# Turning a weight matrix with VectorE and SBUF moves instead of TensorE, in a fused state-space and feed-forward kernel

## The chip, the cores and the metric

The kernel runs on one core of a Trainium2 chip. The metric is the device time of one execution, in microseconds (us). A core has five engines that run side by side: TensorE (PE in the profile; its weight loads are shown apart as PEld), VectorE (DVE), ScalarE (ACT), GpSimd (POOL) and SyncE (SP), which only issues transfers. Sixteen DMA engines carry the transfers that SP, ACT and POOL issue. Matmuls write into PSUM, which has eight banks of 512 f32 numbers on each of 128 partitions; SBUF is the working memory.

## The reference

Two branches of the same input size are mixed by a gate. All sizes: 2048 tokens, model width 448, feed-forward width 1792, state width 448 (complex).

```python
Lam_bar = exp(dt * Lam)                                  # per state lane
Bu   = einsum("bld,pd->blp", x, B_bar)                   # complex
h[t] = Lam_bar * h[t-1] + Bu[t]                          # along 2048 tokens
y    = 2 * einsum("blp,dp->bld", hseq, C).real + x * Dskip
b    = silu(x @ w1) @ w2
g    = sigmoid((x * gate_w).sum(-1))
out  = g * y + (1 - g) * b
```

Inputs and output are bf16. Both branches and the gate take the same x (`A_x`); `B_x` is not used.

## The kernel before

**Tiling.** The tokens are cut into 4 chunks (tc) of 512, and each chunk into 4 blocks (tb) of 128. Weights and x lie in SBUF with the contracted dimension on the partitions. Model width 448 is held as four pieces that overlap (columns 0, 128, 256 and 320), so that products with x use 64-row halves of TensorE, two at a time, into a pair of PSUM banks (line 663). There are two kinds of such product tiles: "F" (x times w1, 14 tiles of 128 features per chunk), which ScalarE evicts with silu into `aT` (line 634), and "B" (x times the turned B, 7 tiles or "slots" per chunk: real and imaginary parts of 448 state lanes), which are copied into a buffer `U`, by VectorE for chunk 0 (line 640) and by ScalarE for the others (line 642). Slot 3 holds 64 lanes of the real and 64 of the imaginary part; two small moves by POOL make its swapped copy, slot 7.

**The recurrence** (`lanes`, line 704 and on). Each lane rotates: the complex recurrence becomes a real one by multiplying U with cosines and sines of the lane's phase (three steps of VectorE: a product with COS into `H`, products with SIN into `PI`, a sum), a scan along the 512 tokens per slot (line 736, into the f32 tile `Gf`), and the rotation back (products with SIN into `PO`, with COS into `H`, a difference). Between scan and rotation back, `Gf` is written as bf16 over U: by POOL transfers (line 390) for chunks 0 to 2, by ScalarE (line 746) for chunk 3. `gin` carries the state into the next chunk. For chunk 0, the first rotation is cut by slot into 18 small steps.

**The readout.** `CP` holds C turned and scaled by the parameters, 7 slots of 128 lanes x 448 columns. For each block, seven matmuls of H with CP (line 795) give y in one PSUM bank, and VectorE adds g times y to `Tb` (line 798), which by then holds g * x * Dskip (line 849) plus the second branch; SP stores the result (line 801). CP is made in `readout_weights`: for each of four slots, 16 TensorE transposes of 56 rows of C (line 814; 64 in all) into a pair of PSUM banks, one or two scaled copies by ScalarE into `ct` (lines 822, 825), and one or two sums by VectorE into CP (lines 827, 830). C itself lies in `H2C`, the space of H of chunk 2, and B in that of chunk 3.

**The second branch.** `ffn2` contracts aT with w2, 14 matmuls per block (line 774); ScalarE scales by 1 - g into `fe` (line 780), and a POOL transfer that accumulates adds fe to Tb (line 782).

**Gates** (`gates`): two products by VectorE, four sums along the row by ScalarE (line 842), tanh and scalings, four scaled copies (line 849).

**The order of the work.** Every operation is recorded with what it reads and writes, a cost and a priority. `Plan.order` then lists it: TensorE keeps the order in which its operations were recorded; each other engine takes, among its operations that could begin soonest, the one with the best priority; PSUM banks are given out in this listing too. The listing fixes each engine's program, and semaphores are placed where one engine needs another. All loads are issued by SP in order (the first few also by ACT): x of chunk 0, w1, parameters, B, gate and Dskip, x of chunk 1, w2, C, x of chunks 2 and 3. The recorded order for TensorE, in short (G is `ffn2`, C the readout, cp the turning of C, xt the turning of x by TensorE, line 508):

```python
x_products(F(0, 0, NH) + B(0) + F(0, NH) + B(1), ...)
for f in cp(0) + G(0, 1) + cp(1, 2) + G(2, 3) + cp(3):
    f()
x_products(F(1) + F(2, 0, 1) + B(2), {2: xt(2, "aa")})
for f in G(4, 5, 6, 7) + C(0, 1, 2, 3):
    f()
x_products(F(2, 1) + B(3) + F(3), {1: xt(3, "aa"), 9: [lambda: gates(3), lambda: lanes(3)]})
for f in C(4, 5, 6, 7) + G(8, 9, 10, 11):
    f()
for f in C(8, 9, 10, 11) + G(12, 13, 14, 15) + C(12, 13, 14, 15):
    f()
```

Of the kernel before, what the change touches and what calls it, by code (L numbers as in the profile page):

```python
# [7 lines left out]
ALU = mybir.AluOpType  # L8
# [6 lines left out]
S_TOK = 2048  # L15
# [9 lines left out]
NFILL = 2  # L25
XCOL = [0, 128, 256, 320]
# [22 lines left out]
class Op:  # L49
    __slots__ = ("i", "eng", "fn", "reads", "writes", "cost", "prio", "sem",  # L50
                 "deps", "succ", "ps_w", "ps_r", "start", "end", "bytes", "tag", "own")


class Plan:
# [5 lines left out]
    RATE = {"pool": 300e3, "hw": 300e3}  # L60
    LAP = {"dve": 0.08, "act": 0.09}
# [6 lines left out]
    def add(self, eng, fn, reads=(), writes=(), cost=0.2, prio=50, sem=None, nbytes=0, tag=""):  # L68
# [28 lines left out]
        o.own = False  # L97
        o.start = o.end = None
# [5 lines left out]
    def order(self):  # L104
# [14 lines left out]
        def earliest(o):  # L119
            t = 0.0  # L120
# [23 lines left out]
        while len(done) < len(ops):  # L144
# [5 lines left out]
            for eng, lst in cands.items():  # L150
# [9 lines left out]
                o = min((c for c in cand if c[0] <= t0 + 1e-9), key=lambda c: (c[1].prio, c[1].i))[1]  # L160
# [116 lines left out]
def bass_gated_mix__ssm_conv_s5__dense_activation_silu__prompt_kernel(nc, A_x, A_Lambda_re, A_Lambda_im, A_B_re, A_B_im, A_C_re, A_C_im,  # L277
               A_log_dt, A_Dskip, B_x, B_w1, B_w2, gate_w, out):
    with ExitStack() as ctx:
# [9 lines left out]
        xT = sb("xT", [128, 4, S_TOK], BF16)  # L289
# [9 lines left out]
        H2C = sb("H2C", [128, 3840], BF16)  # L299
        H = [H2C[:, 0:3584].rearrange("p (s n) -> p s n", s=NSLOT) if k == 2 else sb(f"H{k}", [128, NSLOT, CH], BF16) for k in range(4)]  # L300
        Cnat = H2C[:, :].rearrange("p (b l) -> p b l", b=4)
        cnn = [f"H2_{s}" for s in range(7)] + ["H2_3i"]
# [91 lines left out]
        def load_w1(q, k, a, b):  # L394

            cols = slice(w1cuts[k], w1cuts[k + 1])
            src = B_w1[320:448, cols] if a == 3 else B_w1[128 * a:128 * b, cols].rearrange("(b p) f -> p b f", p=128)
            load(q, w1s[:, 3, cols] if a == 3 else w1s[:, a:b, cols], src, " ".join(f"w1_{k}_{i}" for i in range(a, b)),
                 256 * (b - a) * (cols.stop - cols.start))
# [11 lines left out]
        Bnat = H[3][:, :, 0:D_MOD]  # L411
        load("sp", Bnat[:, 0:3, :], A_B_re[0:384, :].rearrange("(b p) d -> p b d", p=128), "H3_0 H3_1 H3_2", 384 * 896)
        load("sp", Bnat[0:64, 3, :], A_B_re[384:448, :], "H3_3", 64 * 896)
        load("sp", Bnat[64:128, 3, :], A_B_im[384:448, :], "H3_3i", 64 * 896)
        load("sp", Bnat[:, 4:7, :], A_B_im[0:384, :].rearrange("(b p) d -> p b d", p=128), "H3_4 H3_5 H3_6", 384 * 896)
        btn = {s: [f"BT{s}_{h}" for h in range(2)] for s in range(7)}
        load_w1("sp", len(w1cuts) - 2, 0, 3)
        load_w1("sp", len(w1cuts) - 2, 3, 4)
# [8 lines left out]
        def load_C():  # L427

            for h in range(2):
                rows = lambda a: a[224 * h:224 * h + 224, :].rearrange("(b p) l -> p b l", p=56)  # L430
                to = Cnat[64 * h:64 * h + 56]
                load("sp", to[:, :, 0:448], rows(A_C_re), f"Cn0{h} " + (" ".join(cnn) if h == 0 else ""), 224 * 896)
                load("sp", to[:, :, 576:960], rows(A_C_im[:, 0:384]), f"Cn1{h}", 224 * 768)
                load("sp", to[:, :, 448:512], rows(A_C_im[:, 384:448]), f"Cn2{h}", 224 * 300)
                load("sp", to[:, :, 512:576], rows(A_C_re[:, 384:448]), f"Cn3{h}", 224 * 300)
# [32 lines left out]
        def x0_transposes(q0, part, who):  # L468
# [12 lines left out]
            for h in range(2):  # L481
                src = lambda h=h: bk(tk, h).bitcast(BF16)[:, 0:256].rearrange("p (q b n) -> p q b n", q=2, n=64)
                dst = xT[:, q0:q0 + 2, 256 * part:256 * part + 256].rearrange("p q (b h n) -> p q b h n", h=2, n=64)[:, :, :, h, :]
# [11 lines left out]
        xn_of = {tc: {q: [f"xT{tc}_{h}" for h in range(2)] for q in range(4)} for tc in range(1, NCH)}  # L495
        xn_of[0] = {q: [f"xT0_{q}{part}{h}" for part in range(2) for h in range(2)] for q in range(4)}

        def x_transposes(tc, who):
# [13 lines left out]
            for h in range(2):  # L512
                src = lambda h=h: bk(tk, h).bitcast(BF16).rearrange("p (q b n) -> p q b n", q=4, b=4)
                dst = xT[:, :, tc * CH:(tc + 1) * CH].rearrange("p q (b h n) -> p q b h n", h=2, n=64)[:, :, :, h, :]
                if who[h] == "d":
                    DVE(lambda e, src=src, dst=dst: e.tensor_copy(dst, src()), [tk], [f"xT{tc}_{h}"], 0.69, 2.2, "xTe")
                else:
                    ACT(lambda e, src=src, dst=dst: e.activation(dst, src(), AF.Copy), [tk], [f"xT{tc}_{h}"], act_cost(1024), 2.2, "xTe")

# [73 lines left out]
        def b_transposes(s0, s1, who):  # L593
# [12 lines left out]
            PE(mm, [f"H3_{s}" for s in range(s0, s1)] + ["H3_3i"] * (s0 <= 3 < s1) + ["ident"], [tk], n * 4 * 0.0285, "BT")  # L606
# [16 lines left out]
        def evict(pair, tk):  # L623

            kinds = [t[0] for t in pair]
            for k, n in ((0, 2),) if pair[0][:2] == pair[-1][:2] and len(pair) == 2 else ((0, 1), (1, 1))[:len(pair)]:
# [10 lines left out]
                U, un = UG[tc % 2], f"U{tc % 2}_"  # L637
                dst = U[:, sl, :]
                if tc == 0:
                    DVE(lambda e, src=src, dst=dst: e.tensor_copy(dst, src()), [tk], [f"{un}{m}" for m in names], 0.15 + 0.53 * n, 2.6, "U")  # L640
                else:
                    ACT(lambda e, src=src, dst=dst: e.activation(dst, src(), AF.Copy), [tk], [f"{un}{m}" for m in names], act_cost(512 * n), 5, "U")  # L642
# [4 lines left out]
        def x_products(tiles, fill={}, wait=()):  # L647
# [10 lines left out]
            def steps(k, h, a, z):  # L658
                def body(pe):
                    for n, cut in list(enumerate(part[h]))[a:z]:  # L660
                        for b, ((i, p0), tile) in enumerate(zip(cut, pairs[k])):
                            tc = tile[1]
                            r = pe.matmul(bk(toks[k], b), weights(tile, p0, p0 + 64, i), xT[p0:p0 + 64, i, tc * CH:(tc + 1) * CH],  # L663
# [42 lines left out]
        def lanes(tc):  # L706
            pr = 20 + tc
            A, an = H[tc], f"H{tc}"
            U, u = UG[tc % 2], f"U{tc % 2}_"
            Gb = U  # L710
            t = f"L{tc}"
            if tc == 0:
# [20 lines left out]
            for s in (3, 0, 4, 1, 5, 2, 6) if tc else (0, 4, 1, 5, 2, 6, 3):  # L733
# [8 lines left out]
                for dst, src, name in cuts:  # L742
                    if tc + 1 < NCH:
                        load("pool", dst, src, name, 180000, 1, [f"Gf{s}"])
# [23 lines left out]
        def ffn2(tb):  # L768
# [13 lines left out]
            P.add("pool", lambda e: e.dma_start(Tb[:, tb, :], f[:, :], accum_op=ALU.add), [fn, f"Tb{tb}"], [f"Tb{tb}"], 0.94, 2, sem(), 115000, tag="Tb+")  # L782

        outs = [sem() for _ in range(NOT)]

        def readout(tb):
# [3 lines left out]
            for n, (a, b) in enumerate(cuts):  # L790
                tk = Ps()

                def mm(pe, tk=tk, a=a, b=b):
                    for s in range(NSLOT):
                        r = pe.matmul(bk(tk)[:, 0:b - a], H[tc][:, s, o:o + 128], CP[:, s, a:b], start=(s == 0), stop=(s == NSLOT - 1))  # L795
                    return r
                PE(mm, [f"H{tc}_{s}" for s in range(7)] + [f"CP{s}" for s in range(NSLOT)], [tk], NSLOT * (0.0025 + (b - a) / 2400), f"C{tc}")
# [5 lines left out]

        def readout_weights(k):

            tk = Ps(2)

            def mm(pe):
                for j, c0 in ((0, 128 * k), (1, 448 if k == 3 else 576 + 128 * k)):
                    for b in range(4):  # L810
                        o = j * 224 + 56 * b
                        for h in range(2):
                            p = slice(64 * h, 64 * h + 56)
                            r = pe.transpose(bk(tk, h).bitcast(BF16)[:, o:o + 56], Cnat[p, b, c0:c0 + 128], ident[p, p])  # L814
                return r
            PE(mm, [f"Cn{n}{h}" for n in range(4) for h in range(2)] + cnn + ["ident"], [tk], 8 * 0.0285, "CT")
# [102 lines left out]
```

## Time and profile before

| | before |
|---|---|
| median of 3 runs | 141.22 us (141.2 to 141.76) |
| profiled execution | 141.25 us |
| its span in the trace | 139.5 us |
| TensorE clock granted, mean | 0.998 |

The times are of whole executions. The profile is of one execution; its span runs from the first to the last instruction in the trace, so it is a little shorter than the execution's own time. Busy time of an engine is the time in which it had an instruction under way. A line such as L663 is a line of the kernel, and a group of instructions is named by line, engine, operation and the tiles that it writes and reads.

### The profile page before, as it was taken

Reading aid. Unit: us, or ns where it says so; the run is one execution under the profiler, and the core shown is the slowest. Engines: PE = TensorE matmul, PEld = TensorE weight load, DVE = VectorE, ACT = ScalarE, POOL = GpSimd, SP = SyncE. Lnnn points to the kernel's source line nnn. Section 1 sums busy time; section 2 is a strip of 40 time slices with the busy share of each in tenths; the row PEclk is TensorE's granted clock in tenths of the full one; section 3 lists DMA queues with packets and bytes.
Section 4 is the critical chain, followed back from the end, with each engine's and each line's share of the span. In section 5 each row is a group of like instructions: output and inputs, shape, how many; then the busy total and the mean of one; then the engine's idle time right before and its main releaser. Section 6 shows DMA issues by size and latency. Waiting matters only on the chain.

```text
span 139.5 us, 3000 instructions
## 1 busy us (share of the span) xinstructions
PE 135.9 (97%) x1201; PEld 67.0 (48%) x1201; DVE 122.0 (87%) x179; ACT 90.3 (65%) x157; POOL 39.2 (28%) x72
## 2 busy tenths in 40 slices
PE   7999999999999999999999999999999999999992
PEld 2445454455544544455544544444455555555561
DVE  0319999999999999999999999999999999997053
ACT  3349768999989999823694887799931268312300
POOL 7134040100248440227733001824000314022220
PEclk9999999999999999999999999999999999999999
DMA  4998999510156770104976200674202322323242
GB/s 136 337 294 243 363 320 238 177 42 0 31 79 94 129 110 1 38 15 73 157 131 155 38 5 0 95 133 79 38 4 97 66 33 36 83 83 61 40 94 71
DMA packets 17956, 14.71 MB, mean 105 GB/s; under 512 B 2835, under 2 KB 17814, under 8 KB 17942
## 3 DMA queue, kind: packets, MB, share of 16 engines
q0 software_dynamic: 6064, 5.51, 24.8%
q1 hardware_dynamic: 11318, 8.65, 20.7%
q10 hardware_dynamic: 560, 0.36, 0.8%
q8 instruction: 9, 0.15, 0.4%
q14 instruction: 5, 0.04, 0.1%
HBM read 7.17 MB, written 1.84 MB: 65 GB/s over the span
## 4 chain that ended last, share of the span: by engine, by line
PE 97%; DVE 0%; issue 0%
PE ps L663 46%; PE ps L774 31%; PE ps L795 15%; PE ps L463 2%; PE ps L508 1%; PE ps L478 1%; PE ps L814 1%; PE ps L604 1%; DVE ot L798 0%; PE ps L675 0%; PE ps L464 0%; PE ps L536 0%
## 5 line engine op out<-in xcount | busy, mean ns | idle before, releaser
L663 PE MATMUL ps<-xT,w1s 64*128 64x512 bf16 x392 | 48.5, 378 | 0.0
L774 PE MATMUL ps<-w2s,aT 128*128 128x448 bf16 x224 | 43.2, 353 | 0.0
L634 ACT ACTIVATE aT<-ps 128x1024 bf16<-128x1024 f32 (+1 forms) x30 | 28.7, 969 | 8.5 <-PE ps L663 8.4
L774 PEld LDWEIGHTS ps<-w2s,aT 128*128 128x128 bf16 x224 | 21.7, 98 | 20.4 <-ACT xnat L849 0.4
L663 PEld LDWEIGHTS ps<-xT,w1s 64*128 64x128 bf16 x392 | 19.7, 94 | 22.3 <-DVE xT L486 0.7
L663 PE MATMUL ps<-xT,BT 64*128 64x512 bf16 x196 | 25.8, 376 | 0.0
L782 POOL DMA_DIRECT2D xnat<-fe x16 | 14.1, 900 | 37.9 <-ACT fe L780 37.2
L780 ACT ACTIVATE fe<-ps,g 128x448 bf16<-128x448 f32 x16 | 10.1, 632 | 21.1 <-PE ps L774 21.0
L390 POOL DMA_DIRECT2D UG<-Gf x27 | 14.7, 549 | 20.9 <-DVE Gf L736 20.4
L736 DVE TENSOR_TENSOR_SCAN Gf<-rc,gin,H 128x512 f32<-128x512 f32 x14 | 17.2, 1268 | 0.0
L795 PE MATMUL ps<-CP,H 128*128 128x448 bf16 (+2 forms) x98 | 16.4, 326 | 0.0
L663 PEld LDWEIGHTS ps<-xT,BT 64*128 64x128 bf16 x196 | 10.8, 94 | 11.1 <-DVE Gf L562 0.2
L798 DVE SCALAR_TENSOR_TENSOR ot<-ps,g,xnat 128x448 bf16<-128x448 f32 (+2 forms) x18 | 10.8, 622 | 6.0 <-issue 4.6
L390 POOL DMA_DIRECT2D UG<-UG x8 | 4.8, 597 | 29.2 <-ACT UG L642 17.4
L704 DVE TENSOR_TENSOR H<-UG,COS 128x3584 bf16<-128x3584 bf16 (+4 forms) x10 | 12.6, 1266 | 0.0
L795 PEld LDWEIGHTS ps<-CP,H 128*128 128x128 bf16 x98 | 8.9, 98 | 7.5 <-DVE k L752 0.4
L642 ACT ACTIVATE UG<-ps 128x1024 bf16<-128x1024 f32 (+1 forms) x12 | 10.7, 923 | 1.4 <-PE ps L663 1.4
L842 ACT ACTIVATE junk<-xg 128x448 bf16<-128x448 bf16 x16 | 9.2, 574 | 2.1 <-DVE xg L704 2.0
L849 ACT ACTIVATE xnat<-xnat,g 128x448 bf16<-128x448 bf16 x16 | 9.8, 671 | 0.2
L704 DVE TENSOR_TENSOR PI<-UG,SIN 128x512 bf16<-128x512 bf16 (+2 forms) x13 | 9.1, 722 | 0.0
L704 DVE TENSOR_TENSOR PO<-UG,SIN 128x1536 bf16<-128x1536 bf16 (+1 forms) x8 | 8.7, 1087 | 0.1
L736 DVE TENSOR_TENSOR_SCAN Gf<-rc,gin,H2C 128x512 f32<-128x512 f32 x7 | 8.5, 1265 | 0.0
(102 smaller groups left out, 126.5 us busy)
## 6 DMA issues: line engine op xcount, KB each, us to landing
UG<-Gf POOLq DMA_DIRECT2D x21, 128.0 KB, 2.5
xnat<-fe POOLq DMA_DIRECT2D x16, 112.0 KB, 2.6
out_dram<-ot SPq DMA_DIRECT2D x15, 112.0 KB, 1.7
w2s<-in_B_w_dram SPq DMA_DIRECT2D x1, 1568.0 KB, 11.8
xnat<-in_A_x_dram SPq DMA_DIRECT2D x3, 448.0 KB, 6.1
w1s<-in_B_w_dram SPq DMA_DIRECT2D x1, 576.0 KB, 6.2
UG<-UG POOLq DMA_DIRECT2D x8, 64.0 KB, 2.2
H2C<-in_A_C_re_dram SPq DMA_DIRECT2D x2, 196.0 KB
```

The costliest lines, as they stand in the source:

```text
L390: P.add(q, lambda e: e.dma_start(dst, src), list(after), name.split(), 0.6 if q == "pool" else 0.5, prio, sem(), nbytes, tag="ld " + name)
L634: ACT(lambda e, src=src, dst=dst: e.activation(dst, src(), AF.Silu), [tk, "tbl"], [f"aT{tc % 2}_{m}" for m in names], act_cost(512 * n), 2 ...
L642: ACT(lambda e, src=src, dst=dst: e.activation(dst, src(), AF.Copy), [tk], [f"{un}{m}" for m in names], act_cost(512 * n), 5, "U")
L663: r = pe.matmul(bk(toks[k], b), weights(tile, p0, p0 + 64, i), xT[p0:p0 + 64, i, tc * CH:(tc + 1) * CH], start=(h == 0 and n == 0), stop=( ...
L704: DVE(lambda e: e.tensor_tensor(o, a, b, op), r, w, dve_cost(n, 2), prio, tag)
L736: DVE(lambda e, s=s, b=b, init=init: e.tensor_tensor_scan(Gf[:, s, :], rc[:, b:b + 1].to_broadcast([128, CH]), A[:, s, :], init, ALU.mult, ...
L774: r = pe.matmul(bk(tk)[:, 0:D_MOD], aT[tc % 2][:, fb, o:o + 128], w2s[:, fb, :], start=(fb == 0), stop=(fb == NFB - 1))
L780: ACT(lambda e: e.activation(f[:, :], bk(tk)[:, 0:D_MOD], AF.Copy, scale=g1[:, tb:tb + 1]), [tk, f"g1_{tc}"], [fn], act_cost(448, 1), 7, "fe")
L782: P.add("pool", lambda e: e.dma_start(Tb[:, tb, :], f[:, :], accum_op=ALU.add), [fn, f"Tb{tb}"], [f"Tb{tb}"], 0.94, 2, sem(), 115000, tag= ...
L795: r = pe.matmul(bk(tk)[:, 0:b - a], H[tc][:, s, o:o + 128], CP[:, s, a:b], start=(s == 0), stop=(s == NSLOT - 1))
L798: DVE(lambda e, tk=tk, a=a, b=b: e.scalar_tensor_tensor(ot[tb % NOT][:, a:b], bk(tk)[:, 0:b - a], g[:, tb:tb + 1], Tb[:, tb, a:b], ALU.mul ...
L849: ACT(lambda e, tb=tb: e.activation(Tb[:, tb, :], xnat[:, tb, :], AF.Copy, scale=g[:, tb:tb + 1]), [f"xd{tc}", f"g_{tc}"], [f"Tb{tb}"], ac ...
```

## The change

What it does, part by part:

- **C is turned without TensorE.** Its six loads put 128 rows to a block (`Cnat`, in the space of H of chunk 2, the last block's lower half zeroed by POOL), ahead of w2. In `readout_columns`, VectorE turns the 32x32 squares of each block (four instructions of 128x896) into the third U buffer, and 16 SP transfers carry the squares to their place in CP, as runs of 32 bf16 numbers. ScalarE and VectorE then scale CP in place as before, from SBUF instead of PSUM.
- **A third U buffer**, and three H buffers instead of four: chunk 3 takes H and U of chunk 0. B lies in the third U buffer before it is turned.
- **Slots 2 and 3 of chunk 0's U** are copied by ScalarE; the others stay with VectorE (`UDVE`).
- **Chunk 0's first rotation** runs in four large steps like the other chunks' (`L0M`).
- **The sums of blocks 4 to 11** (`OUTA`): ScalarE copies g times y as f32 into `ct`, a POOL transfer accumulates it into Tb, and SP stores Tb.
- **The order**: the readouts of chunks 0 and 1 come behind the last run of products, chunk 3's lanes are recorded behind the readout of chunk 0, x of chunk 1 is turned one pair earlier, and several priorities and transfer costs of the listing change.
- x turned lies by chunk (`xT[:, tc, i, :]`), CP has a slot pitch of 512, and the last cut of w1 is loaded in two halves. `x_blocks` is new but not used (`XBLK` is empty).

```diff
+L0M = True
+XT1K = 6
+XBLK = ()
+UDVE = (0,1,4,5,6)
+OUTA = tuple(range(4,12))
+CPRIO = 2.9
+CPP = 20.5
+CTAT = 59.0
+GPR = (14, 20.3, 21.5, 19)
+CASTB = (360000,360000,360000)
...
-        xT = sb("xT", [128, 4, S_TOK], BF16)
+        xT = sb("xT", [128, NCH, 4, CH], BF16)
-        CP = sb("CP", [128, NSLOT, D_MOD], BF16)
+        CP = sb("CP", [128, NSLOT, CH], BF16)
-        UG = [sb(f"UG{k}", [128, 8, CH], BF16) for k in range(2)]
+        UG = [sb(f"UG{k}", [128, 8, CH], BF16) for k in range(3)]
-        H2C = sb("H2C", [128, 3840], BF16)
...
+        H = [sb(f"H{k}", [128, NSLOT, CH], BF16) for k in range(3)]
+        Cnat = H[2][:, :, :].rearrange("p s n -> p (s n)").rearrange("p (b l) -> p b l", b=4)
...
-        Bnat = H[3][:, :, 0:D_MOD]
+        Bnat = UG[2][:, :, 0:D_MOD]
...
+            n = 0
+            for b0, b1, p in ((0, 3, 128), (3, 4, 64)):
+                rows = lambda a: a[128 * b0:128 * b0 + p * (b1 - b0), :].rearrange("(b p) l -> p b l", p=p)
+                for dst, src in (((0, 448), rows(A_C_re)), ((512, 896), rows(A_C_im[:, 0:384])), ((448, 512), rows(A_C_im[:, 384:448]))):
+                    load("sp", Cnat[0:p, b0:b1, dst[0]:dst[1]], src, f"Cn{n}" + (" " + " ".join(cnn) if n == 0 else ""),
+                         p * (b1 - b0) * max(300, 2 * (dst[1] - dst[0])), None, ["Cnz"] * b0)
...
+        POOL(lambda e: e.memset(Cnat[:, 3, :], 0.0), [], ["Cnz"], 0.9, 5)
         load_xn(1)
+        load_C()
         load("sp", w2s[:, :, :], B_w2.rearrange("(fb p) d -> p fb d", p=128), "w2", F_FF * 896)
-        load_C()
...
-                if tc == 0:
+                if tc == 0 and a in UDVE:
                     DVE(lambda e, src=src, dst=dst: e.tensor_copy(dst, src()), [tk], after, 0.15 + 0.53 * n, 2.6, "U")
...
-            if tc == 0:
+            if tc == 0 and not L0M:
...
+                if tb in OUTA:
+                    f, fn = ct[tb // 2 % 2][:, tb % 2, :], f"ct{tb // 2 % 2}{'ab'[tb % 2]}"
+                    ACT(lambda e, tk=tk, f=f: e.activation(f, bk(tk)[:, 0:D_MOD], AF.Copy, scale=g[:, tb:tb + 1]),
+                        [tk, f"g_{tc}"], [fn], act_cost(448, 1), 3, "out")
+                    P.add("pool", lambda e, f=f: e.dma_start(Tb[:, tb, :], f, accum_op=ALU.add), [fn, f"Tb{tb}"], [f"Tb{tb}"], 0.94, 2, sem(), 300000, tag="Tb+")
+                    P.add("sp", lambda e: e.dma_start(out2[t0:t0 + 128, :], Tb[:, tb, :]), [f"Tb{tb}"], [], 0.3, 1, outs[NOT], 128 * 896, tag="st")
+                    continue
...
+        def readout_columns():
+
+            C32 = UG[2][:, 0:NSLOT, :].rearrange("p s n -> p (s n)").rearrange("p (m t b i) -> p m t b i", m=4, b=4, i=32)
...
+            for b in range(4):
+                src = Cnat[:, b, :].rearrange("p (t m i) -> p t m i", m=4, i=32)
+                dst = C32.rearrange("p m t b i -> p b t m i")[:, b, :, :, :]
+                DVE(lambda e, dst=dst, src=src: e.transpose(dst, src), [f"Cn{n}" for n in range(6)] + ["Cnz"] + [CBEH] * (CBEH != "") + cnn + turned, [names[b]],
+                    0.15 + 896 / 960, CPRIO, "CTd")
+            k = sem()
+            for g in range(4):
+                for m in range(4):
+                    to = CP[32 * m:32 * m + 32, :, :].rearrange("p t (b g i) -> p (t b) g i", b=4, i=32)[:, :, g, :]
+                    P.add("sp", lambda e, to=to, g=g, m=m: e.dma_start(to, C32[32 * g:32 * g + 32, m, :, :, :].rearrange("p t b i -> p (t b) i")),
+                          names + held, [f"CT{g}{m}"], 0.75, 400, k, 300000, tag="CTm")
...
         def readout_weights(k):
 
-            tk = Ps(2)
-
-            def mm(pe):
-                for j, c0 in ((0, 128 * k), (1, 448 if k == 3 else 576 + 128 * k)):
...
-                            r = pe.transpose(bk(tk, h).bitcast(BF16)[:, o:o + 56], Cnat[p, b, c0:c0 + 128], ident[p, p])
...
+            re, im = CP[:, k, 0:D_MOD], CP[:, 4 + k, 0:D_MOD] if k < 3 else None
...
+            DVE(lambda e: e.scalar_tensor_tensor(re, re, sc1[:, k:k + 1], c[:, 0, :], ALU.mult, ALU.add),
+                ctn + ["sc1"] + both, [f"CP{k}"], 0.68, CPP, "CP")
...
-        for f in cp(0) + G(0, 1) + cp(1, 2) + G(2, 3) + cp(3):
+        for f in G(0, 1, 2, 3):
             f()
+        for f in cp(0, 1, 2, 3):
+            f()
...
-        for f in G(4, 5, 6, 7) + C(0, 1, 2, 3):
+        for f in G(4, 5, 6, 7):
             f()
-        x_products(F(2, 1) + B(3) + F(3), {1: xt(3, "aa"), 9: [lambda: gates(3), lambda: lanes(3)]})
-        for f in C(4, 5, 6, 7) + G(8, 9, 10, 11):
+        x_products(F(2, 1) + B(3) + F(3), {1: xt(3, "aa") if 3 not in XBLK else [], 9: [lambda: gates(3)]})
+        for f in C(0, 1, 2, 3):
             f()
-        for f in C(8, 9, 10, 11) + G(12, 13, 14, 15) + C(12, 13, 14, 15):
+        lanes(3)
+        for f in C(4, 5, 6, 7) + G(8, 9, 10, 11, 12, 13) + C(8, 9, 10, 11) + G(14, 15) + C(12, 13, 14, 15):
             f()
```

More of the change, by code (lines that the diff above doesn't have):

```diff
@@ L50 @@
     __slots__ = ("i", "eng", "fn", "reads", "writes", "cost", "prio", "sem",
-                 "deps", "succ", "ps_w", "ps_r", "start", "end", "bytes", "tag", "own")
+                 "deps", "succ", "ps_w", "ps_r", "start", "end", "bytes", "tag", "own", "at")
 class Plan:
@@ L97, in add @@
         o.own = False
+        o.at = 0.0
         o.start = o.end = None
@@ L826, in readout_weights @@
                 both.append(cn + "b")
-            DVE(lambda e: e.scalar_tensor_tensor(in_two(CP[:, k, :]), re(), sc1[:, k:k + 1], in_two(c[:, 0, :]), ALU.mult, ALU.add),
-                [tk, "sc1"] + both, [f"CP{k}"], 0.68, 1, "CP")
+            else:
+                for a, b in ((slice(0, 64), slice(64, 128)), (slice(64, 128), slice(0, 64))):
+                    ACT(lambda e, a=a, b=b: e.activation(c[a, 0, :], CP[b, 3, 0:D_MOD], AF.Copy, scale=sc2[b, 3:4]), ctn + ["sc2"], [cn + "a"], act_cost(448, 1), 8, "ct").at = CTAT
```

125 lines of the change are left out of this document (71 added, 54 removed).

## The prediction

> **What bounds the kernel now.** I read the page first, then TensorE's waits, then the chain of waits in order of time.
>
> ```profile
> span 139.5 us, 3000 instructions
> PE 135.9 (97%) x1201; PEld 67.0 (48%) x1201; DVE 122.0 (87%) x179; ACT 90.3 (65%) x157; POOL 39.2 (28%) x72
> ...
> PE 97%; DVE 0%; issue 0%
> ```
>
> TensorE is busy for 97% of the span, and the chain that ended last lies on it for 97% too. Busy time alone proves little, since ends of matmuls are modelled, so the waits of TensorE come next (line, releaser, total us, times, longest):
>
> ```profile
> PE ps L463 <- PEq L904: 0.8, 1, 0.8
> ```
>
> That is TensorE's only wait in the whole run, at its start. So the time now is TensorE's list of work, added up: a change gains what it takes off this list, and loses what new waits on it cost. VectorE (87%) is the next most loaded engine. The chain (start us, us, what) shows the work in question:
>
> ```profile
> 28.31 0.21 PE ps L814 x16
> 28.51 5.40 PE ps L774 x28
> 33.92 0.52 PE ps L814 x32
> 34.44 5.40 PE ps L774 x28
> 39.84 0.31 PE ps L814 x16
> 40.15 5.40 PE ps L663 x50
> ...
> 57.24 10.70 PE ps L774 x56
> ...
> 73.24 3.99 PE ps L663 x36
> ...
> 131.38 5.35 PE ps L795 x42
> ```
>
> L814 are the 64 small transposes of C, L774 the second feed-forward product, L663 the products with x, L795 the readout. The pieces abut.
>
> **The change part by part.**
>
> *TensorE.* The 64 transposes go: 0.21 + 0.52 + 0.31 = 1.04 us. Do the neighbours change? Two L774 pieces of 28 with C between them cost 5.40 + 5.40 = 10.80, one of 56 behind products costs 10.70: 0.10 more saved. But the product piece behind them will start behind L774 instead of behind transposes. The piece at 73.24, behind full-height matmuls, takes 3.99 for 36, where the one at 40.15 would take 5.40 x 36/50 = 3.89: 0.10 lost. They cancel; I keep 1.04, with bounds 0.9 and 1.15. All other matmuls stay in number and size; the readouts of chunks 0 and 1 move behind the long run of products, and the turning of x for chunk 1 one pair forward.
>
> *VectorE gets four 32x32 transposes of 128x896.* In the changed kernel's instruction order they stand behind the copy of x and ahead of the last phase step of slot 2. The trace has no such transpose; the nearest rows (count | busy, mean ns):
>
> ```profile
> L640 DVE CAST UG<-ps 128x1024 bf16<-128x1024 f32 x3 | 3.6, 1216 | 0.0
> L736 DVE TENSOR_TENSOR_SCAN Gf<-rc,gin,H 128x512 f32<-128x512 f32 x14 | 17.2, 1268 | 0.0
> L565 DVE COPY COS<-COS 128x1536 bf16<-128x1536 bf16 x1 | 0.5, 531 | 0.0
> ```
>
> As fast as the copy: 531 x 896/1536 = 0.3 us; as slow as the scan: 1268 x 896/512 = 2.2 us. I take the cast, the row for one element after the other: 1216 x 896/1024 = 1.1 us, 4.4 us for four. Queued behind them is that last phase step (L562), from which ScalarE makes a cosine, and behind the cosine, in order, a copy out of PSUM that frees the bank of the first L774 tile.
>
> ```profile
> 20.50 0.68 DVE L516 COPY xT<-ps 128x1024 bf16<-128x1024 bf16 x1
> 21.10 0.68 DVE L527 TENSOR_TENSOR Gf<-Gf 128x512 f32<-128x512 f32 x1
> 21.70 0.48 DVE L555 TENSOR_SCALAR Gf<-aT,ph 128x512 f32<-128x512 f32 x1
> 22.09 0.42 DVE L562 TENSOR_SCALAR Gf<-Gf 128x512 int32<-128x512 int32 x1
> ```
>
> ```profile
> 23.10 0.71 ACT L563 ACTIVATE COS<-Gf,hpi 128x512 bf16<-128x512 f32 x1
> ...
> 54.32 0.59 ACT L642 ACTIVATE UG<-ps 128x512 bf16<-128x512 f32 x1
> ```
>
> The cosine is done at 23.81 now. Four transposes add 4.4, the pair copy that leaves VectorE takes 1.2 away, and L527 and L555, which stood between the copy of x and L562, now come earlier (22.09 - 21.10 = 1.0): 26.0. A copy of 0.6 behind it ends at 26.6, and TensorE wants the bank at 28.3: 1.7 us are left, so nothing is lost up to 1.5 us per transpose.
>
> *Sixteen moves by SP* carry the 32x32 blocks to their place, each 32 partitions x 28 runs of 64 B: 14,336 runs, 896 for each of 16 DMA engines. The trace has no 64 B run. The windows 17 to 18 us (long packets only) and 21 to 23 us (short ones mixed in) bound it (packets, MB, share of 16 engines):
>
> ```profile
> q1 hardware_dynamic: 425, 0.38, 108.9%
> ```
>
> ```profile
> DMA packets 865, 0.42 MB, mean 212 GB/s; under 512 B 490, under 2 KB 847, under 8 KB 865
> ...
> q1 hardware_dynamic: 830, 0.35, 91.0%
> ```
>
> Long packets of 896 B take 16 x 1.089 us / 425 = 41.0 ns. In the mixed window a packet takes 16 x 2 x 0.91 / 830 = 35.1 ns; with its 340 long ones at 41.0, the 490 short ones (mostly 128 B, pieces of C) take at most (29.1 - 13.9) / 490 = 31 ns. From below, SP's issuing is the limit, 0.66 us for each of these two, 10.6 us for 16:
>
> ```profile
> 18.70 1.32 SPq L390 DMA_DIRECT2D H2C<-in_A_C_im_dram  x2
> ```
>
> So the moves last between 10.6 and 896 x 35.1 = 31.4 us. They start at about 26: the transposes end near 25 (the copy of x at 20, a short copy, four times 1.1), and the loads ahead of the moves drain then, as the window shows, whose last two columns are DMA share and GB/s. A small move within SBUF needs 2.2 us to land:
>
> ```profile
> 26.00:28.00 2.00, 2.00 (x22) 0.93 (x20) 2.00 (x7) 2.00 (x4) 0.79 (x2) 1.00 0.24 83
> ```
>
> ```profile
> UG<-UG POOLq DMA_DIRECT2D x8, 64.0 KB, 2.2
> ```
>
> Who waits? The turned blocks lie in the third U buffer, so ScalarE's first copy of chunk 2 into it (now at 54.32, then at 53.3) waits for all 16 moves. 128 B take at most 31 ns, a run has half the bytes; I take 20 ns: 26 + 17.9 + 2.2 = 46. That is hidden with 7 us to spare and costs nothing. The moves show from (53.3 - 26 - 2.2) / 896 = 28 ns a run.
>
> The Trainium skill, "DMA: Bandwidth & Descriptors", Specifications, asks for 512 B per transfer for line rate and says that smaller ones are read, modified and written back. By that rule the sum would be that of rival two; the mixed window, with 31 ns at most for a short packet against 41.0 for a long one, neither shows nor excludes it.
>
> *The loads.* C now comes ahead of w2, and both ahead of x of chunks 2 and 3. The same bytes are done near 26 as now, and w2, no longer last but before 0.9 MB of x, is wanted at 28.3. The first transpose wants C near 20.
>
> ```profile
> 9.59 0.44 SPq L390 DMA_DIRECT2D xnat<-in_A_x_dram  x1
> ```
>
> ```profile
> xnat<-in_A_x_dram SPq DMA_DIRECT2D x3, 448.0 KB, 6.1
> ```
>
> x of chunk 1 lands at 9.6 + 6.1 = 15.7; C's 0.8 MB behind it need 2.2 us at the long packets' rate (0.38 MB in 1 us), 3.8 at the mixed window's 212 GB/s: 17.9 to 19.5, in time. A late C would hold VectorE's next copy out of PSUM.
>
> *VectorE's balance.* Its last work before the final readout:
>
> ```profile
> 126.07 2.09 DVE L704 TENSOR_TENSOR H<-H,PO 128x2048 bf16<-128x2048 bf16 x2
> ```
>
> ```profile
> L798 DVE SCALAR_TENSOR_TENSOR ot<-ps,g,xnat 128x448 bf16<-128x448 f32 x15 | 9.9, 673 | 5.9 <-issue 4.6 <-PE ps L795 1.3
> L704 DVE TENSOR_TENSOR H<-UG,COS 128x3584 bf16<-128x3584 bf16 x4 | 8.0, 2006 | 0.0
> L704 DVE TENSOR_TENSOR PI<-UG,SIN 128x512 bf16<-128x512 bf16 x7 | 2.7, 416 | 0.0
> ```
>
> It ends at 128.2, 3.2 us ahead of TensorE's 131.38. Eight sums leave (8 x 0.673 = 5.4), one pair copy (1.2), and in chunk 0's rotation seven small products (2.7) and seven adds of their size become large steps (2.0 each at the 3584 row): 1.4. That is 8.0 less and 4.4 more; with TensorE 1.0 earlier, 3.2 + 3.6 - 1.0 = 5.8 us are spare. The seven CP sums stay. Chunk 3's rotation now waits for the readouts of chunk 0, whose buffer it takes over. Behind those TensorE still has three readout groups (5.35 each, one of them the final) and six or two L774 tiles between them: 5.3 + 15.9 + 5.3 + 5.3 = 31.8 us to the final readout, against 7 x 1.27 of scans and six large steps of 2.0, 20.9. All of this covers, and gains nothing by itself.
>
> *ScalarE* gets eight copies of readout sums and one pair copy.
>
> ```profile
> 110.23 0.63 ACT L780 ACTIVATE fe<-ps,g 128x448 bf16<-128x448 f32 x1 [2.02 <-PE ps L774]
> ```
>
> A copy of 0.63 per readout tile of 1.33 us fits, and around them it idles 2 us per L774 tile. Pool's eight added accumulations and their stores run beside it and end before the final readout, whose tail stays as it is.
>
> The sum: 141.25 (span 139.5, and 1.75 around it) - 1.04 = 140.2. The median of the runs shown, 141.22, is the profiled time within 0.03, so nothing is corrected.
>
> **The rivals.**
>
> *One: ScalarE becomes the bound in the long run of products.* The gates of chunk 2, which stood under L774 and the readout, now fall into the run of 34 product tiles:
>
> ```profile
> 31.30 0.58 ACT L842 ACTIVATE junk<-xg 128x448 bf16<-128x448 bf16 x1
> ...
> 36.99 2.37 ACT L849 ACTIVATE xnat<-xnat,g 128x448 bf16<-128x448 bf16 x4
> ...
> 78.19 1.93 ACT L518 ACTIVATE xT<-ps 128x1024 bf16<-128x1024 bf16 x2
> 80.00 1.96 ACT L634 ACTIVATE aT<-ps 128x1024 bf16<-128x1024 f32 x2
> ```
>
> ScalarE: 17 pairs x 0.98 + 1.9 + 8 gate sums x 0.58 + 2.4 = 25.6, and the small steps of two gates on top. TensorE: 238 matmuls at 5.40/50 = 25.7, and 32 small transposes. For it: a full stretch. Against: some gate sums can run after the products, and with four pairs of banks TensorE runs about 1 us ahead. Price 0.3 to 1.2 us: 140.5 to 141.4, about no change.
>
> *Two, on the other side: the moves come late.* If a 64 B run costs 35.1 ns, they land at 26 + 31.4 + 2.2 = 59.6, 6.3 us after ScalarE wants the buffer. Behind its waiting copy stand the other copies of chunk 2, the gates and the fe copies; the banks stay full and TensorE stops at the next L774 group. With about 1.3 us of cover, 5 us: 145.2. At 41.0 ns it would be 36.7 us of moves and 150.5. It decides from 28 ns up; for it the mean of the mixed window, against it the 31 ns that bound even 128 B there.
>
> *Three: slow transposes.* At 2.2 us each, the 4.4 us beyond those taken pass through the cosine and the copy to TensorE's bank, less 1.7 of cover: 2.7 lost, 142.9. It decides from 1.5 us. The Trainium skill, "VectorE: DVE Perf Modes", The three transpose paths, gives 311 ns for a 128x128 block; seven of those make an estimate of 2.2 us for 896 columns, and the sum would be this rival's. No row here shows a transpose on VectorE.
>
> **How the numbers follow.** Forecast (TensorE unbroken): 0.58, 139.9 to 140.5. Rival one 0.22, rival two 0.10, rival three 0.10 (140.5 to 142.9 by the transposes' length). A measurement of this kernel tells about 0.5% (0.7 us) from no change. Faster by more than that is the forecast alone, 0.58; within it, rival one and the mild end of rival three, 0.26; slower, rival two and the rest of three, 0.16. The range 139.8 to 142.0 holds the forecast, rival one and half of rival three.
>
> **What would show it.** Right: no transposes of C on the chain, one L774 piece of 56 between 28 and 39, TensorE's only wait still the first, the end of its list near 135.7, transposes near 1.1 us, the moves landed before 53. Wrong: a TensorE wait near 28 (slow transposes or late C), at 55 to 57 behind ScalarE's copies of chunk 2 (moves), several short ones between 66 and 93 (ScalarE), or chunk 3's H steps ending after TensorE reaches the final readout.

## The result and the profile after

| kernel | median of its executions, us | ratio to the kernel before, 95% interval |
|---|---|---|
| before, 6 executions | 141.36 | |
| after, 6 executions | 140.31 | 0.9925 [0.9901, 0.9949] |
| after, 11 more, another chip | 141.13 (before beside it: 141.80) | 0.9919 [0.9886, 0.9952] |

The change gains 1.06 us in the first comparison (0.75% of 141.36) and 1.15 in the second, and both intervals lie under 1. Forecast were 140.2 us and a gain of 1.04. Some executions of every kernel run in a slower state; a ratio leaves them out and a median does not, so the ratios carry the verdicts.

The page of the kernel after: span, busy time, and the share of the chain that ended last.

```profile
span 138.9 us, 2883 instructions
...
PE 135.2 (97%) x1137; PEld 66.0 (48%) x1137; DVE 119.2 (86%) x160; ACT 96.3 (69%) x167; POOL 46.8 (34%) x81
...
PE 96%; DVE 1%; issue 0%; DVEq 0%
```

TensorE's waits in the kernel after:

```profile
PE ps L486 <- PEq L968: 0.8, 1, 0.8
```

The bound is the same as before, a list of TensorE work with one wait at its start, and that list has 64 instructions less. The chain (start us, us, what) shows the change in place:

```profile
9.26 0.18 PE ps L580 x4
...
28.74 10.70 PE ps L819 x56
39.44 5.50 PE ps L708 x50
...
71.79 21.80 PE ps L708 x202
93.59 10.70 PE ps L840 x56
104.29 15.89 PE ps L819 x84
...
130.77 3.99 PE ps L840 x21
```

The second feed-forward product of chunk 0 (L819) is one piece where three pieces of transposes cut it before, and the readouts of chunks 0 and 1 (93.59) stand behind the long run of products. This execution took 140.68 us, 0.37 more than the median. Its trace shows a late start: the four small parameter matmuls (L580) came later than in the kernel before, whose chain has this row:

```profile
8.82 0.18 PE ps L536 x4
```

The 30 product matmuls ahead of them took 4.25 us here and 3.82 in the kernel before. In eleven of the runs below, TensorE's waits list one for a load of w1 there, of 0.4 to 1.7 us, so the start differs from execution to execution. So I compare a **stretch** that leaves the start out: from the first of these matmuls (by the instructions' own starts, 8.76 before and 9.19 after, a little ahead of the chain's) to the final readout (131.38 and 130.77). It is 122.62 us before and 121.58 after: 1.04 less. The tail behind it, to the end of the last sum by VectorE, is 5.72 us in both.

### The profile page after: what moved, and what is told of

Read it like the earlier page. It is cut to its first block, busy times and chain, and to the rows that moved or that the text cites. A ratio compares the mean times of both kernels' runs of the same rounds, so it can differ in the third digit from the quotient of the medians.

```text
span 138.9 us, 2883 instructions
## 1 busy us (share of the span) xinstructions
PE 135.2 (97%) x1137; PEld 66.0 (48%) x1137; DVE 119.2 (86%) x160; ACT 96.3 (69%) x167; POOL 46.8 (34%) x81
## 4 chain that ended last, share of the span: by engine, by line
PE 96%; DVE 1%; issue 0%; DVEq 0%
PE ps L708 47%; PE ps L819 31%; PE ps L840 14%; PE ps L486 2%; DVE ot L850 1%; PE ps L533 1%; PE ps L501 1%; PE ps L648 1%; PE ps L720 0%; PE ps L487 0%; PE ps L580 0%; DVEq L289 0%
## 5 line engine op out<-in xcount | busy, mean ns | idle before, releaser
L819 PE MATMUL ps<-w2s,aT 128*128 128x448 bf16 x224 | 43.0, 353 | 0.0
L819 PEld LDWEIGHTS ps<-w2s,aT 128*128 128x128 bf16 x224 | 21.8, 98 | 20.9 <-issue 0.8
L781 DVE TENSOR_TENSOR_SCAN Gf<-rc,gin,H 128x512 f32<-128x512 f32 x21 | 25.4, 1264 | 0.1
L840 PE MATMUL ps<-CP,H 128*128 128x448 bf16 (+2 forms) x126 | 21.7, 332 | 0.0
L407 POOL DMA_DIRECT2D UG<-Gf x27 | 15.8, 660 | 15.7 <-DVE Gf L781 15.5
L840 PEld LDWEIGHTS ps<-CP,H 128*128 128x128 bf16 x126 | 11.6, 98 | 10.0 <-DVE xnat L749 0.4
L749 DVE TENSOR_TENSOR H<-UG,COS 128x3584 bf16<-128x3584 bf16 (+2 forms) x9 | 16.1, 1810 | 0.0
L687 ACT ACTIVATE UG<-ps 128x1024 bf16<-128x1024 f32 (+1 forms) x13 | 11.9, 938 | 0.5 <-PE ps L708 0.5
L850 DVE SCALAR_TENSOR_TENSOR ot<-ps,g,xnat 128x448 bf16<-128x448 f32 (+2 forms) x10 | 5.7, 585 | 7.5 <-issue 6.2
L847 POOL DMA_DIRECT2D xnat<-ct x8 | 6.9, 866 | 6.7 <-ACT ct L845 6.6
L845 ACT ACTIVATE ct<-ps,g 128x448 f32<-128x448 f32 x8 | 5.1, 634 | 5.7 <-PE ps L840 5.7
L749 DVE TENSOR_TENSOR PI<-UG,SIN 128x1536 bf16<-128x1536 bf16 (+1 forms) x8 | 8.5, 1085 | 0.0
```

The source lines that it names most:

```text
L407: P.add(q, lambda e: e.dma_start(dst, src), list(after), name.split(), 0.6 if q == "pool" else 0.5, prio, sem(), nbytes, tag="ld " + name)
L749: DVE(lambda e: e.tensor_tensor(o, a, b, op), r, w, dve_cost(n, 2), prio, tag)
L781: DVE(lambda e, s=s, b=b, init=init: e.tensor_tensor_scan(Gf[:, s, :], rc[:, b:b + 1].to_broadcast([128, CH]), A[:, s, :], init, ALU.mult, ...
L819: r = pe.matmul(bk(tk)[:, 0:D_MOD], aT[tc % 2][:, fb, o:o + 128], w2s[:, fb, :], start=(fb == 0), stop=(fb == NFB - 1))
L840: r = pe.matmul(bk(tk)[:, 0:b - a], H[tc % 3][:, s, o:o + 128], CP[:, s, a:b], start=(s == 0), stop=(s == NSLOT - 1))
```

## The experiments

The stretch in all runs, with the time's ratio to the kernel before that was measured beside it:

| run | stretch, us | ratio, 95% interval |
|---|---|---|
| before | 122.62 | |
| after; after_again | 121.58; 121.58 | 0.9925; 0.9919 |
| e1_turns_back | 122.63 | 0.9978 [0.9950, 1.0006] |
| e2_before_no_turns | 122.34 | 0.9948 [0.9913, 0.9983] |
| e2b_late_copies | 121.85 | 0.9933 [0.9901, 0.9964] |
| e3_sums_dve | 121.59 | 0.9937 [0.9909, 0.9965] |
| e4_dve_relief_undone | 123.35 | 1.0097 [1.0067, 1.0128] |
| e5c_moves_24 | 121.59 | 0.9917 [0.9880, 0.9953] |
| e5_moves_doubled | 126.11 | 1.0322 [1.0270, 1.0374] |
| e5b_moves_tripled | 138.84 | 1.1067 [1.1017, 1.1118] |
| e6_transposes_doubled | 125.48 | 1.0181 [1.0145, 1.0216] |
| e7_x3_blocks; e7b_x3_blocks | 121.12; 121.12 | 0.9949; 0.9943 |

An interval reaches 0.3 to 0.7 us to each side; the stretch repeated to 0.01 us in the two kernels that were profiled twice. The theory is that of the prediction, TensorE's list. The main rival: the gain came from the relief of VectorE and ScalarE.

### The kernel after once more

> The kernel after, unchanged, beside the next three on one chip, since the times of the first eight came from two chips on which it did not run. Theory: 0.9 to 1.2 us under the kernel before in the mean of many executions, and in the trace 1.05 us less from the small parameter matmuls near 9 us to the final readout. Rival (part of the first comparison was the start, whose waits for the first loads differ from execution to execution): 0.3 to 0.7 us under.

The theory holds: 0.9919, and the same stretch to the hundredth, though its parameter matmuls came at 9.79. The start moves the whole, not the stretch.

### The transposes put back

```diff
-        for f in G(0, 1, 2, 3):
+        gh = [lambda k=k: ghost(k) for k in range(4)]
+        for f in gh[:1] + G(0, 1) + gh[1:3] + G(2, 3) + gh[3:]:
```

`ghost(k)` records 16 transposes of rows of w1.

> The kernel after, plus 64 TensorE transposes of 56 rows that turn rows of w1 for nothing, of the size and number of those that the change removed and at the same four places among the first four groups of the second feed-forward product; each group of 16 is read by one ScalarE activation of one column (about 0.2 us). Nothing else is added, and VectorE still turns C. Theory (TensorE's list is the time): the 1.04 us come back, 1.0 to 1.2 us over the kernel after, 141.3 to 141.5, equal to the kernel before. Rival (the gain came from the relief of VectorE and ScalarE or from the new order, and the transposes stood in time that was free): no more than 0.3 us over the kernel after, 140.3 to 140.6.

The chain of this run has the three pieces again (L887), and the final readout at 134.11:

```profile
31.03 0.21 PE ps L887 x16
...
36.65 0.52 PE ps L887 x32
...
42.57 0.31 PE ps L887 x16
...
134.11 3.99 PE ps L841 x21
```

Its parameter matmuls started late, at 11.48, behind a wait for w1 and 3.4 us at half of the clock (0.50 from 8 to 10 us). The stretch leaves that out: it is 122.63, 1.05 over the kernel after, and that of the kernel before to 0.01. The ratio, 0.9978, agrees with no gain. So with everything else of the change in place, the transposes alone cost what was forecast.

### The transposes taken from the kernel before

```diff
-            PE(mm, [...] + cnn + ["ident"], [tk], 8 * 0.0285, "CT")
...
+            tk = [...] + cnn + ["w1_0_0", "w1_0_1", "w1_1_0", "w1_1_1"]
+            re = lambda: in_two(w1s[:, 0, 0:D_MOD])
+            im = lambda: in_two(w1s[:, 1, 0:D_MOD])
```

> The kernel before without its 64 transposes and with nothing in their place: the columns of the readout are scaled from rows of w1 that lie in SBUF, so the turning of C is left out. No move, no third U buffer, no change of order or of engines. Theory (the list): the whole gain of the change without any of its other parts, 0.9 to 1.15 us under the kernel before, 140.2 to 140.45. Rival (the gain came from the other parts): within 0.3 us of the kernel before, 141.1 to 141.5.

By its size this is the rival: the stretch is only 0.28 shorter, of the 1.04 that the theory asked for. The ratio, 0.2 to 1.2 us under the kernel before, does not tell the two apart. TensorE's waits and the chain of this run:

```profile
PE ps L663 <- ACT aT L634: 0.6, 1, 0.6
```

```profile
38.92 2.60 DMA xnat<-fe
41.59 0.05 issue
41.63 0.63 ACT fe L780
...
42.82 0.92 ACT aT L634
43.74 0.05 issue
43.79 1.69 PE ps L663 x14
```

Read upward: a product tile waits for a bank that ScalarE has not copied out (aT), that copy stands behind `fe`, and fe waits for a POOL transfer to free its buffer. The seven scaled copies for CP, free of TensorE, had moved ahead of the gates, and the gates release those transfers. So ScalarE became the bound in this stage. Was it the order, or is ScalarE full there? The next run puts the seven copies behind (the lines with `ACT` are against the run above):

```diff
-        for f in cp(0) + G(0, 1) + cp(1, 2) + G(2, 3) + cp(3):
+        for f in G(0, 1, 2, 3) + cp(0, 1, 2, 3):
...
-            ACT(..., tk + ["sc2"], [cn + "a"], act_cost(448, 1), 3, "ct")
+            ACT(..., tk + ["sc2", "fe0", "fe1"], [cn + "a"], act_cost(448, 1), 22, "ct")
```

> The kernel before without its 64 transposes, as in the earlier run (the turning of C is left out), but with ScalarE's seven scaled copies for the readout weights behind its four copies of the second branch of chunk 0, instead of ahead of the gates. The earlier run gained 0.28 us of 1.04 in the stretch from the parameter matmuls to the final readout, and TensorE waited 0.59 us for ScalarE at 43.8. Theory (the list, with ScalarE's order as the lost part): that wait is gone, the stretch is 121.5 (1.04 under the kernel before), and the time 0.9 to 1.1 us under it. Rival (ScalarE is full from 22 to 44 whatever its order, and the gain of the change needs the copies that it lost there): a wait of 0.3 us or more stays, and the gain is 0.2 to 0.6.

That wait is gone and the stretch is 121.85: 0.77 of 1.04, between the theory and the rival. The last 0.27 hangs on ScalarE still, now on its copies of turned x, by the chain:

```profile
45.57 0.91 ACT aT L634
46.48 1.84 ACT xT L518 x2
48.37 8.38 PE ps L663 x76
```

So mostly the order. Whether the rest is order or fullness stays open, since two of the seven copies still stand ahead of this stage's product tiles, at 41.2 to 42.5. In the kernel after the copies for CP come behind 60, and ScalarE waits for TensorE in this stage (0.49 us ahead of the copy of a product tile):

```profile
43.48 1.02 ACT L678 ACTIVATE aT<-ps 128x1024 bf16<-128x1024 f32 x1 [0.49 <-PE ps L708]
...
60.61 0.66 ACT L882 ACTIVATE ct<-CP,scc 128x448 f32<-128x448 bf16 x1
```

### VectorE's relief undone, in part and whole

```diff
-OUTA = tuple(range(4,12))
+OUTA = ()
```

> The kernel after with the eight f32 sums of blocks 4 to 11 put back on VectorE. This adds 8 x 0.67 = 5.4 us to VectorE, which ended 4.8 us ahead of the final readout in the kernel after, while sums that come early may find gaps. Theory (the other parts are covered and gain nothing by themselves): 0 to 0.6 us over the kernel after, 140.3 to 140.9. Rival (the sums carry the gain): 1 us or more over the kernel after, 141.3 or more.

The stretch is 121.59. VectorE's last work before the final readout, then the readout's piece on the chain:

```profile
131.23 2.09 DVE L749 TENSOR_TENSOR H<-H,PO 128x2048 bf16<-128x2048 bf16 x2
```

```profile
133.38 5.52 PE ps L840 x42
```

It ends at 133.32, 0.06 us ahead. In the kernel after the same work left 4.8 us (its two rows; the second has the idle time before it in brackets):

```profile
123.91 2.08 DVE L749 TENSOR_TENSOR H<-H,PO 128x2048 bf16<-128x2048 bf16 x2
132.19 0.69 DVE L850 SCALAR_TENSOR_TENSOR ot<-ps,g,xnat 128x448 bf16<-128x448 f32 x1 [6.20 <-issue]
```

So the eight sums use up the spare time and cost nothing yet; the tail is 0.17 longer. The other two edits go with them in the next run:

```diff
-L0M = True
+L0M = False
-UDVE = (0,1,4,5,6)
-OUTA = tuple(range(4,12))
+UDVE = tuple(range(7))
+OUTA = ()
```

> The kernel after with all of VectorE's relief undone: the eight f32 sums back (5.4 us), the two slots of the first Bu back (1.2), and chunk 0's first rotation cut by slot again (1.4 shorter as large steps were dearer). Some 5 to 7 us more on VectorE against 4.8 us that it ended ahead of the final readout in the kernel after. Theory (the relief gains nothing by itself but carries the added transposes): 0.5 to 2.5 us over the kernel after, 140.8 to 142.8, with the loss as a wait of TensorE for VectorE ahead of the final readout and none earlier. Rival (the relief is not needed at all): within 0.3 us of the kernel after, 140.1 to 140.6.

The theory's loss at the place that it named:

```profile
PE ps L840 <- DVE H L749: 1.8, 1, 1.8
```

The stretch is 1.77 longer, and the time slower than before by 1.0% [0.7, 1.3]. The relief gains nothing by itself (the kernel with the transposes put back had it, and no gain), but without it the added transposes turn the gain into a loss.

### More moves

```diff
-                    P.add("sp", lambda e, ...: e.dma_start(to, C32[...]...),
-                          names + held, [f"CT{g}{m}"], 0.75, 400, k, 300000, tag="CTm")
+                    fr = C32[...]...
+                    for a, z in ((0, 16), (16, 32)):
+                        P.add("sp", lambda e, to=to[:, :, a:z], fr=fr[:, :, a:z]: e.dma_start(to, fr),
+                              names + held, [f"CT{g}{m}_{a}"], 0.375, 400, k, 150000, tag="CTm")
```

> The kernel after with each of the 16 moves cut into two, 32 moves of 28,672 runs of 32 B. By the 0.77 us of SP per move in the trace of the kernel after they end at 25.1 + 32 x 0.77 + 2.4 = 52.2, still ahead of ScalarE's first copy of chunk 2 at 53.5. Theory (the moves are hidden, and their length is that of SP's issuing): no change, within 0.3 us of the kernel after. Rival (the moves take their time from something else that runs beside them, the other transfers or the runs themselves): 0.5 us or more over it.

The theory's forecast of no change fell, with its end of the moves: the loss is the rival's. SP's rows, in the kernel after and then in this run:

```profile
25.11 12.31 SPq L873 DMA_DIRECT2D CP<-UG  x16
```

```profile
25.77 32.30 SPq L875 DMA_DIRECT2D CP<-UG  x32
```

A move costs 0.77 us of SP in the mean with 16, but 1.01 with 32. The chain of this run names the dear ones:

```profile
38.08 0.04 issue
38.12 0.99 SPq L875
...
47.09 3.35 SPq L875
50.45 0.04 issue
50.49 3.37 SPq L875
...
57.41 2.28 DMA CP<-UG
```

From 38 to 54 some take up to 3.4 us, and in 43 to 54 the DMA engines are fully used (share 1.04, against 0.65 in the kernel after): POOL's transfers of the scans run there too. The moves landed at 59.7, and TensorE paid (ScalarE's copy with its idle time, TensorE's wait, and the feed-forward piece behind it):

```profile
59.76 0.60 ACT L687 ACTIVATE UG<-ps 128x512 bf16<-128x512 f32 x1 [5.47 <-DMA CP<-UG]
```

```profile
PE ps L819 <- ACT UG L687: 3.1, 1, 3.1
```

```profile
60.41 12.08 PE ps L819 x56
```

ScalarE is 5.5 us late, TensorE waits 3.14 of it, and its piece takes 12.08 instead of 10.70. 3.14 + 1.38 = 4.52; the stretch grew by 4.53. The granted clock explains the second term (PE busy, and behind it PEclk, DMA share, GB/s):

```profile
60.00:61.00 1.00, 0.59 (x2) 0.29 (x3) 1.00 (x1) 1.00 (x4) 0.35 (x1) 0.50 0.00 0
...
63.00:64.00 1.00, 1.00 (x6) 0.54 (x5) 1.00 (x2) 1.00 (x3) 0.00 (x0) 0.94 0.00 0
```

Up to 63.1 it is 0.50: 2.7 us of the piece at half of the clock, worth 1.4. Three pieces for each move make the same larger:

```diff
+                    for a, z in ((0, 16), (16, 24), (24, 32)):
```

> The kernel after with each of the 16 moves cut into three (16, 8 and 8 columns), 48 moves of 43,008 runs. By 0.77 us of SP per move they end at 25.1 + 37 + 2.4 = 64.4, 11 us after ScalarE's first copy of chunk 2 wants the third U buffer. Theory (late moves are what the change risked: the price is the lateness less some 1.3 us of cover in PSUM banks): 7 to 10 us over the kernel after, 147 to 150, as a wait of TensorE in the products of chunk 2. Rival (ScalarE has other work to go on with, or the moves are issued faster when they are smaller): 0 to 3 us over it.

```profile
PE ps L819 <- ACT UG L687: 14.6, 1, 14.6
```

```profile
70.88 13.40 PE ps L819 x56
```

14.55 + 2.70 = 17.25, and the stretch grew by 17.26. In both runs TensorE's wait is 2.3 us less than the time that ScalarE stood idle for the moves (5.47 and 16.89): that is the cover, where 1.3 was expected. The mechanism of the theory holds; its size was too small, as the moves ended at 70. Does it start with more moves, or only with late ones?

```diff
+                    for a, z in (((0, 32),) if m % 2 else ((0, 16), (16, 32))):
```

> The kernel after with every second of the 16 moves cut into two, 24 moves. With 32, SP needed 0.66 us for each of the first 17, but 1.2 to 3.4 us for some of those issued between 43 and 54, where POOL's transfers of the scans run, and ended at 58. Theory (the moves cost nothing as long as they are issued before that stretch): 24 moves end at 25.3 + 24 x 0.75 = 43.3, landed by 46, and the time is that of the kernel after within 0.3 us. Rival (more runs slow the scans' transfers or the copies of the second branch, whenever they end): 0.4 us or more over it.

```profile
25.54 22.34 SPq L875 DMA_DIRECT2D CP<-UG  x24
```

The issuing ends at 47.9, 4.6 us later than I expected. The last move is issued at 45.8 and needs 9.4 us to land, so ScalarE's first copy of chunk 2 waits for it:

```profile
55.28 0.60 ACT L687 ACTIVATE UG<-ps 128x512 bf16<-128x512 f32 x1 [1.21 <-DMA CP<-UG]
```

TensorE has no wait there, and the stretch is that of the kernel after, to 0.01. So 24 moves are late already, by 1.2 us, and the cover of 2.3 us hides it; the time holds as the theory said, though the moves landed at 55 and not by 46. With 16 the last lands at 40.8, some 13 us ahead of ScalarE's copy at 53.5. Moves cost nothing until they are later than the cover, and that point lies between 24 and 32 of them.

### The transposes doubled

```diff
-            for b in range(4):
+            for b in (0, 0, 1, 1, 2, 2, 3, 3):
```

> The kernel after with each of VectorE's four transposes done twice, one after the other into the same place: 4 x 1.08 = 4.3 us more on VectorE at 20 to 25 us; one short step of the second slot's phase moves ahead of the last of them in VectorE's order. Theory (about 1.7 us are spare from the transposes through a cosine and a copy out of PSUM to TensorE's bank at 28.7): 1.3 to 2.6 us over the kernel after, 141.6 to 142.9, as a wait of TensorE at the first tiles of the second feed-forward product near 29. Rival (VectorE's spare time, 4.8 us at the end, takes it up, since nothing near 28 hangs on it): 0 to 0.3 us over it.

TensorE's waits, and ScalarE's cosine behind the transposes:

```profile
PE ps L840 <- ACT aT L678: 1.5, 1, 1.5
PE ps L819 <- ACT UG L687: 1.5, 1, 1.5
...
PE ps L708 <- ACT fe L825: 0.6, 1, 0.6
```

```profile
28.14 0.72 ACT L607 ACTIVATE COS<-Gf,hpi 128x512 bf16<-128x512 f32 x1 [3.79 <-DVE Gf L606]
```

The place was right, but the delay is paid in two more places: the three waits make 3.6, and the stretch grew by 3.90, not by 1.3 to 2.6. The third, ahead of L840, comes at 95: ScalarE stands idle for 3.9 us in front of a gate sum whose product VectorE makes at 94.33 (89.83 in the kernel after), with product tiles to copy behind it. VectorE's spare time at the end of the program is not to be had in its middle.

### x of chunk 3 turned by VectorE too

```diff
-XBLK = ()
+XBLK = (3,)
```

> The kernel after with x of chunk 3 also turned by VectorE and moved to its place by SP, where the kernel after turns it with 32 TensorE transposes. This takes another 32 transposes off TensorE (32 x 1.04/64 = 0.5 us) and two pair copies off ScalarE, and adds transposes of 32x32 squares to VectorE ahead of chunk 2's products. Theory (the list): 0.4 to 0.6 us under the kernel after, 139.7 to 139.9. Rival (VectorE's added time or the late moves turn into a wait): no gain, 140.3 to 141.

> The same kernel as in the earlier run with x of chunk 3 turned by VectorE, now beside the kernel after on one chip. In the first trace the stretch from the parameter matmuls to the final readout was 121.05 us against 121.51 in the kernel after, but the executions were longer outside the span than those of other kernels. Theory (the list): 0.3 to 0.6 us under the kernel after in the same call. Rival (what was saved is lost outside that stretch): no difference, or up to 0.5 us over it.

The long run of products has lost its transposes in both chains (the row is of the first run; the second has the same length):

```profile
67.64 25.79 PE ps L708 x238
```

The stretch is 121.12 both times, 0.46 under the kernel after. The time shows no gain: 0.9949 [0.9914, 0.9983] and 0.9943 [0.9905, 0.9982]. The second lies above the 0.9919 of the kernel after, which ran beside it, with intervals that overlap. So the stretch came as the theory said, and the time as the rival did. In 12 of its 24 executions the time outside the span was over 2.0 us (up to 3.2), where the kernel after had 1.75 to 1.83 in all 11. What lengthens it lies outside of what the trace shows and stays open. It is no version that is shown to beat the kernel after.

## Why the prediction was right, step by step

- **TensorE's list, 1.04 us: right.** The stretch is 1.04 shorter, and the transposes put back cost 1.05. The neighbours cancel as said: the products behind the feed-forward piece take 5.50 instead of 5.40, and that piece 10.70 instead of 10.80. Median 140.31 against 140.2.
- **"All of this covers, and gains nothing by itself": right for VectorE.** The sums back on VectorE cost 0.01 in the stretch, and with all of its relief undone the loss is 1.8.
- **ScalarE between 27 and 48: not priced.** The transposes taken out without the other parts gain 0.28, with the seven copies late 0.77. The whole 1.04 came only in the kernel after, where none of these copies stands in that stage. The prediction looked at ScalarE's new copies and at the long run of products alone; that TensorE stayed unbroken here came true without having been worked out.
- **The transposes, 1.1 us: right.** The group in the kernel after:

```profile
L867 DVE STREAM_TRANSPOSE UG<-H 128x896 bf16<-128x896 bf16 x4 | 4.2, 1083 | 0.0
```

  The cover of 1.7 us was nearer 1.3: doubled, they delayed the cosine by 2.8 (counted from the parameter matmuls) and TensorE, at its first wait, by 1.5. The rival of slow transposes was priced too low: 2.7 lost for 4.4 more, where 4.3 more lost 3.9, since I followed the delay to its first victim only. The estimate from the Trainium skill ("VectorE: DVE Perf Modes", The three transpose paths), 2.2 us, is twice the measured time.
- **The moves: hidden, as said, but by more, and for another reason.** Forecast from 26 to 46 at 20 ns a run; they were issued from 25.1 to 37.4, and the last landed at 40.8. In 31 to 36 us, with nothing but short packets (count, MB, share of 16 engines):

```profile
q1 hardware_dynamic: 5583, 0.35, 59.8%
```

  16 x 5 x 0.598 / 5583 = 8.6 ns a packet. The prediction's lower bound was the limit, SP's issuing: 16 moves in 12.3 us, with the DMA engines at 60%. Rival two's 35.1 ns a run did not come. The Trainium skill ("DMA: Bandwidth & Descriptors", Specifications) wants 512 B for line rate, and the trace agrees that short packets are slower by the byte: 64 B in 8.6 ns are 7.4 bytes per ns, where the loads' 896 B in 41.0 ns are 21.9. The same page of the Trainium skill, Why small descriptors are slow (HBM only), says that transfers within SBUF are spared the penalty of small ones; these numbers do not show that. Late moves cost about what rival two said, 4.5 us for 5.5 late, but as 3.1 of waiting and 1.4 of clock; its cover of 1.3 us, worked out from no row, was 2.3.
- **C lands in time: right.** VectorE starts the first transpose at 20.41 without idle time.
- **VectorE's spare time: 4.8 us, forecast 5.8.** The mis-sized term is its balance; nothing hung on it.
- **ScalarE in the long run of products: no wait**, against rival one.

## What to carry to other kernels

Where an engine's list is the time, price a change by what leaves the list, then look which engine comes next in that stage: the same 64 instructions were worth 0.28, 0.77 or 1.04 us, by how ScalarE's work lay beside them. Compare executions from an instruction behind the start, if the start waits for loads. Follow an added delay past its first victim: in-order engines pass it on to stages where the spare time of the program's end is not at hand.

## What was not expected of the hardware

- TensorE's granted clock fell to 0.50 in waits of 3.1 and 14.6 us and stayed there for 2.7 and 5.4 us behind them, which cost 1.4 and 2.7 us on top. It also fell to 0.50, for 3.4 us, behind waits of only 1.4 us (e1) and 1.7 us (e3) near 6 us, ahead of the stretch; waits of 1.5 us (e6) and 1.8 us (e4) left it at 1.00. The Trainium skill, "TensorE: Matmul & The Clock Gate", Part 1, has the clock fall to half after an idle window of about 3.4 us. The waits of 14.6 us and of 1.5 and 1.8 agree with that; the falls at 1.4, 1.7 and 3.1 us do not follow from it. So the length of a wait alone does not decide, and what does is not shown.
- Most of SP's issues of a move took 0.66 us, at a DMA share of 0.5 to 0.7, and some up to 3.4 us between 38 and 54, at a share near 1. The share alone does not decide it: the kernel before issued two loads in 0.66 us each at 18.7, at a share of 1.14. What holds the issuer there is not shown.
